# A planned instruction order laid out again, with separate hold and result times: cross-covariance attention followed by a channel mix

## The chip, the cores and the metric

One core of a Trainium2 chip runs the whole kernel. The metric is the device time of one execution in microseconds (us); lower is better. Three runs of the kernel before gave a median of 528.32 us (528.12 to 529.24).

## The reference

Cut to what matters, with B = 4, N = 6208, C = 256 and a hidden width of 1024:

```python
# attention over channels: per batch a 256 x 256 matrix
qn = q / (norm(q, axis=1) + 1e-6);  kn = k / (norm(k, axis=1) + 1e-6)
a  = softmax(kn.T @ qn / tau)
x  = v @ a
# channel mix
xk = mu_k * x + (1 - mu_k) * x_prev      # x_prev: x one row later, zero at row 0
xr = mu_r * x + (1 - mu_r) * x_prev
out = sigmoid(xr @ w_r) * (relu(xk @ w_k) ** 2 @ w_v)
```

The matrix `a` of a batch needs all rows of q and k of that batch, so the covariance of a batch must be complete before the first row of its x can be computed.

## The kernel before

The kernel does not issue instructions as its loops go. It first writes a list of steps with `add(engine, duration, key, function, reads, writes)` (class `Plan`). A step depends on the last writer of what it reads and on the readers of what it overwrites. Then `Plan.order()` lays all steps out in a small model of the machine: at each point the engine that can start first takes, of its steps whose inputs are there, the one with the lowest key. The keys say when a step is due: block n has its due time around n * T. The steps are then issued in the order of their modelled starts, and each engine runs its own list strictly in that order on the chip.

In the model of before a step holds its engine for one duration, and its result is there when that duration is over, plus a wait that depends on the engine that uses it (`WAIT`: PE 0.3, ACT and DVE 0.12, POOL 0.15). The durations are `act(n) = 0.17 + n/1200`, `dve(n) = 0.16 + n/960/mode`, `pe(n) = n/2400 + 0.0025`.

The work is tiled as follows. Batch 0 is special: its q and k come in as float32 over SP's queue (`ld0`, L280), DVE casts them (L291), ACT or DVE squares them (L300, L297), and TensorE accumulates the covariance (`cov0`, L313, into `s_ps`) and the sums of squares (`nq0` L306, `nk0` L319, into `vr`). There `s0` is a ring of three squared tiles, and `rq` (L324, L239 to L267) turns the norm of q into a row of factors. The function `softmax` then makes the matrix: copy of the norm of k (L365), a power on POOL (L239), two small DVE steps (L241, L244), two products with `rq` (L372), two exponentials on ACT (L386), and the two halves of `A` (L391, L393).

After that the kernel runs over 49 blocks, 48 of them of 512 rows (one of 256 holds the rests of the four batches). Each block goes through these steps:

- v is loaded by POOL's queue as bf16 (`v_load`, L335, ring `v_bf` of four) and transposed, the first five blocks on TensorE (`v_turn_pe`, L351, copied by DVE at L353), the others by a DMA on SP's queue (`v_turn_dma`, L341).
- `x_stage`: four matmuls of 512 columns make x in two halves (L427, into `xp`), each evacuated into `xR`, mostly by ACT (L437).
- `mix_stage` on DVE: difference `dl` (L467), products with mu `dm` (L475), sums `xk` and `xr` (L484).
- `up_stage`: four pairs of hidden tiles, each pair four matmuls of 512 columns (L513) into one of the two buffers `kT`; ACT takes the relu of the pair (L516, into `kr`, a ring of three), DVE squares it (L518, into `kk`).
- `down_stage`: for each 128 rows two gate matmuls (L546) and eight down matmuls (L551) into one of the two buffers `vr`; ACT takes a tanh (L555), DVE multiplies (L557), SP's queue stores (L571).

Between the blocks of one batch the covariance of the next batch is accumulated (`cov_group`): q and k are loaded by POOL's queue as bf16 (L622), ACT squares both at once (`sq`, L634, 128 x 2048), DVE adds twice (L637, L640), TensorE makes the covariance (`cov`, L650) and the sums (`norm`, L657), DVE adds these up (L664).

Of the kernel before, what the change touches and what calls it, by code (L numbers as in the profile page):

```python
# [13 lines left out]
OP = mybir.AluOpType  # L14
# [3 lines left out]
class Step:  # L18
    __slots__ = ("eng", "dur", "out", "key", "fn", "deps", "users", "left", "ready", "start", "seq", "size", "name")


class Plan:
# [3 lines left out]
    WAIT = {"PE": 0.3, "ACT": 0.12, "DVE": 0.12, "POOL": 0.15, "SP": 0.0}  # L26

    def __init__(self):
        self.steps = []
        self.writer = {}  # L30
        self.readers = {}

    def add(self, eng, dur, key, fn, reads=(), writes=(), size=0, name="", after=()):
        s = Step()
        s.eng, s.dur, s.key, s.fn, s.size, s.name = eng, dur, key, fn, size, name
        s.seq = len(self.steps)
        s.deps, s.users = set(after), []
        for r in reads:
            if r in self.writer:
                s.deps.add(self.writer[r])  # L40
            self.readers.setdefault(r, []).append(s)
        for w in writes:
            if w in self.writer:
                s.deps.add(self.writer[w])
            for r in self.readers.get(w, ()):
                s.deps.add(r)
            self.writer[w] = s
            self.readers[w] = []
        s.deps.discard(s)
        self.steps.append(s)  # L50
        return s

    RATE = 395e3
    MOVE = 1.3
    LAND = 0.8

    def order(self):
        import heapq
        for s in self.steps:
            s.left = len(s.deps)  # L60
            s.ready = 0.0
            for d in s.deps:
                d.users.append(s)
        free = {e: 0.0 for e in self.WAIT}
        waiting = {e: [] for e in self.WAIT}
        able = {e: [] for e in self.WAIT}
        bus = 0.0
        for s in self.steps:
            if s.left == 0:
                heapq.heappush(waiting[s.eng], (0.0, s.seq, s))  # L70
        done = []
        while len(done) < len(self.steps):
            best = None
            for e in free:
                if able[e]:
                    t = free[e]
                elif waiting[e]:
                    t = max(free[e], waiting[e][0][0])
                else:
                    continue  # L80
                if best is None or t < best[0]:
                    best = (t, e)
            t, e = best
            while waiting[e] and waiting[e][0][0] <= t:
                _, q, s = heapq.heappop(waiting[e])
                heapq.heappush(able[e], (s.key, q, s))
            s = heapq.heappop(able[e])[2]
            s.start = t
            end = t + s.dur
            free[e] = end  # L90
            if s.size:
                bus = max(bus, end + self.MOVE) + s.size / self.RATE
                end = bus + self.LAND
            s.out = end
            done.append(s)
            for u in s.users:
                lag = 0.0 if s.size else (0.02 if u.eng == e else self.WAIT[e])
                u.ready = max(u.ready, end + lag)
                u.left -= 1
                if u.left == 0:  # L100
                    heapq.heappush(waiting[u.eng], (u.ready, u.seq, u))
        done.sort(key=lambda s: (s.start, s.seq))
        return done


def pe(n):
    return n / 2400 + 0.0025


def act(n, ptr=0):  # L110
    return 0.17 + n / 1200 + 0.09 * ptr


def dve(n, mode=1):
    return 0.16 + n / 960 / mode
# [3 lines left out]
def kernel(  # L119
# [89 lines left out]
    T = 9.7  # L209
# [26 lines left out]
    def inverse(i, key, srcn, sres, lo, hi, name):  # L236

        nres = ("nq" if lo == 0 else "nk", i)
        add("POOL", 0.8, key + .01, lambda: nc.gpsimd.tensor_tensor(nrm[i][:, lo:hi], srcn[:, lo:hi], half[:, lo:hi], op=OP.pow),  # L239
            reads=[(sres, i)], writes=[nres], name=name + " pow")  # L240
        add("DVE", dve(4), key + .02, lambda: nc.vector.tensor_scalar_add(nrm[i][:, lo:hi], nrm[i][:, lo:hi], 1e-6),  # L241
            reads=[nres], writes=[nres], name=name)
        rw = [("rrq", i)] if hi == 2 else [("rrk", i)] if lo == 2 else [("rrq", i), ("rrk", i)]
        add("DVE", dve(4), key + .03, lambda: nc.vector.reciprocal(rr[i][:, lo:hi], nrm[i][:, lo:hi]),  # L244
            reads=[nres], writes=rw, name=name)
        if inv_tau != 1.0 and hi == 4:
            add("DVE", dve(4), key + .03, lambda: nc.vector.tensor_scalar_mul(rr[i][:, 2:4], rr[i][:, 2:4], inv_tau),
                reads=[("rrk", i)], writes=[("rrk", i)], name=name)

    def spread(i, key, name):  # L250
# [3 lines left out]
        add("DVE", dve(2), key + .04, lambda: nc.vector.tensor_copy(h, rr[i][:, 0:2]), reads=[("rrq", i)], writes=w, name=name)  # L254
        add("DVE", dve(2), key + .05, lambda: nc.vector.tensor_tensor(rd[i], rr[i][:, 0:2], h, op=OP.subtract),
            reads=[("rrq", i)] + w, writes=[("rd", i)], name=name)
        add("DVE", dve(2), key + .06, lambda: nc.vector.tensor_copy(m, rd[i]), reads=[("rd", i)], writes=w, name=name)
        add("DVE", dve(2), key + .07, lambda: nc.vector.tensor_tensor(l, rd[i], m, op=OP.subtract),
# [7 lines left out]
        add("PE", 6 * pe(P), key + .08, go, reads=w, writes=[("xp",)], name=name)  # L266
# [5 lines left out]
    for i, (tn, g, j0, j1) in enumerate(order0):  # L272
# [29 lines left out]
        if tn == "q":  # L302
            for j in range(j0, j1):
# [4 lines left out]
                add("PE", 0.13, key + 0.3, go, reads=[("s0", si)], writes=[("vr", 1)], name="nq0")  # L308
        else:
            for j in range(j0, j1):  # L310
# [4 lines left out]
                add("PE", 2 * pe(C), key + 0.1, go, reads=[cres, ("q0", g % NQ0)], writes=[("s_ps",)], name="cov0")  # L315
# [5 lines left out]
                add("PE", 0.16, key + 0.2, go, reads=[("s0", si)], writes=[("vr", 0)], name="nk0")  # L321
        if tn == "q" and g == NB:
            kq = key + 0.6
            add("DVE", dve(2), kq, lambda: nc.vector.tensor_copy(nrm[0][:, 0:2], vr[1][:, 0:2]),  # L324
                reads=[("vr", 1)], writes=[("nq", 0)], name="rq")
            inverse(0, kq, nrm[0], "nq", 0, 2, "rq")
            spread(0, kq, "rq")
# [11 lines left out]
    def v_turn_dma(n, key):  # L339
# [3 lines left out]
            reads=[("v_bf", i)], writes=[("vT", o)], size=M * C * 8, name="turn v")  # L343

    def v_turn_pe(n, key, pb, other=None):
# [6 lines left out]
        add("PE", 8 * 0.06, key, go, reads=[("v_bf", i)], writes=[pb[1]] + ([other] if other else []), name="turn v")  # L352
# [9 lines left out]
    def softmax(b, key, s_key):  # L362
        i = b % 2
        if b == 0:
            add("DVE", dve(2), key, lambda: nc.vector.tensor_copy(nrm[i][:, 2:4], vr[0][:, 0:2]),  # L365
# [14 lines left out]
        for ih in range(2):  # L380
# [7 lines left out]
            add("ACT", act(C, 1) + 0.19, key + .13 + .01 * ih, go, reads=[("rrk", i), ("mx", i)],  # L388
                writes=[("e", i, ih), ("sm", i, ih)], name="chain exp")
        for ih in range(2):  # L390
            add("DVE", dve(2), key + .15 + .01 * ih, lambda ih=ih: nc.vector.reciprocal(sm[i][:, ih:ih + 1], sm[i][:, ih:ih + 1]),  # L391
                reads=[("sm", i, ih)], writes=[("sm", i, ih)], name="chain")
            add("DVE", dve(C, 1.5), key + .155 + .01 * ih, lambda ih=ih: nc.vector.tensor_scalar_mul(  # L393
# [12 lines left out]
    def x_stage(n, key):  # L406
# [11 lines left out]
        for ci, (c0, c1) in enumerate(cuts):  # L418
            for dh in range(2):
# [11 lines left out]
                def both(go=go, kx=kx, w=c1 - c0, dh=dh, c0=c0, c1=c1, dst=dst, dres=dres):  # L431
                    add("PE", 2 * pe(w), kx, go, reads=[("A", b, 0), ("A", b, 1), ("vT", o)], writes=[dres], name="x")
# [8 lines left out]
    def mix_stage(n, key):  # L441
# [6 lines left out]
        for c0, c1 in cuts:  # L448
# [20 lines left out]
            unit(kd, lambda dgo=dgo, kd=kd, w=w: add("DVE", dve(2 * w, 2) + (.16 if left else 0), kd, dgo, reads=xdep,  # L469
                                                    writes=[("dl", di)], name="delta"))  # L470
            for which in "kr":
                km = kd + (.02 * T if which == "k" else .3 * T)
                for dh in range(2):
                    col = dh if which == "k" else 2 + dh
                    unit(km, lambda col=col, dh=dh, c0=c0, c1=c1, km=km, w=w: add("DVE", dve(w, 4), km, lambda: nc.vector.tensor_scalar_mul(  # L475
# [10 lines left out]
                unit(km + .01, lambda mgo=mgo, km=km, w=w, res_=res_: add("DVE", dve(2 * w, 2) + (.16 if left else 0), km, mgo,  # L486
# [16 lines left out]
    def up_pair(n, p, c0, c1, w, ku):  # L503
        def go():
# [3 lines left out]
            for x in range(2):  # L508
# [6 lines left out]
                marks[n] = add("PE", 2 * pe(w), ku + x * .02, mm, reads=[("w_k",), ("xk", n % 2, c0)], writes=[("kT", bk, x)], name="up")  # L515
# [19 lines left out]
    def down_tile(n, s, kd, last):  # L535
# [3 lines left out]
        def go():  # L539
# [7 lines left out]
            add("PE", 2 * pe(D), kd, gate, reads=[("xr", ri), ("w_r",)], writes=[("vr", bk)], name="gate")  # L547
            for p in range(4):
# [4 lines left out]
                add("PE", 2 * pe(D), kd + .01 * p, dn, reads=[("kk", n % 2, p, c0), ("w_v",)], writes=[("vr", bk)], name="down")  # L553
# [3 lines left out]
            add("DVE", 0.15 + D / 960, kd + .4, lambda: nc.vector.scalar_tensor_tensor(  # L557
# [24 lines left out]
    def left_stage(b, key):  # L582
# [13 lines left out]
        def both():  # L596
            add("PE", 4 * pe(65), kl, go, reads=[("A", b, 0), ("A", b, 1), ("vlT", i)], writes=[("xp",)], name="x left")
# [15 lines left out]
    def cov_group(b, g, key, dk):  # L613
# [12 lines left out]
        def work():  # L626
# [20 lines left out]
            for s in range(n):  # L647
# [4 lines left out]
                add("PE", 2 * pe(C), key + s * dk, go, reads=both, writes=[("s_ps",)], name="cov")  # L652
# [6 lines left out]
            add("PE", 0.3, kn, go, reads=[wres], writes=[("xp",)], name="norm")  # L659
            ai = b % 2  # L660
            if g == 0:
                add("DVE", dve(4), kn + .1, lambda: nc.vector.tensor_copy(acc[ai], xp[:, 0:4]), reads=[("xp",)], writes=[("acc", ai)], name="norm")
            else:
                add("DVE", dve(4), kn + .1, lambda: nc.vector.tensor_tensor(acc[ai], acc[ai], xp[:, 0:4], op=OP.add),  # L664
# [24 lines left out]
    add("DVE", dve(4), KC + .01, lambda: nc.vector.tensor_copy(mu, vr[1][:, 0:4]), reads=[("vr", 1)], writes=[("mu",)], name="mu")  # L689
# [83 lines left out]
```

## Time and profile before

| what | value |
|---|---|
| median of three runs | 528.32 us |
| span of the profiled execution, first to last instruction | 526.0 us |
| median of the runs less the span | 2.3 us |
| TensorE (PE) busy | 491.1 us, 93% of the span |
| VectorE (DVE) busy | 417.8 us, 79% |
| ScalarE (ACT) busy | 398.5 us, 76% |
| GpSimd (POOL) busy | 88.7 us, 17% |
| share of the chain of work that ended last that lies on PE | 77% |

How to read it: the span runs from the first to the last instruction of one execution, and some 2.3 us of the measured time lie around it. A matmul's busy time reaches to the arrival of its result, and the next matmul starts before that; so the busy share of PE is not its distance from its best rate. What counts is where PE waited, for what, and what the granted clock was. The profiled execution's own total time is not given beside its span; where a time of the whole kernel is worked out from the span, the 2.3 us are added.

### The profile page before, as it was taken

How to read it: one execution, taken by the hardware profiler on the slowest of the kernel's cores; microseconds unless marked ns; L12 is line 12 of the kernel's file. 1: busy time of each engine (PE TensorE's matmuls, PEld its weight loads, DVE VectorE, ACT ScalarE, POOL GpSimd, SP SyncE). 2: the span in 40 equal slices, each digit the busy share in tenths (PEclk: the TensorE clock that was granted, in tenths of full speed). 3: DMA queues.
4: the chain of work that ended last, by engine and by line, in shares of the span. 5: the costliest groups of instructions: out<-in, count | busy, mean ns of one | idle time of the engine just before them, and what ended most of it. 6: DMA issues, size and time to landing. Idle time of an engine off the chain costs nothing.

```text
span 526.0 us, 9943 instructions
## 1 busy us (share of the span) xinstructions
PE 491.1 (93%) x3707; PEld 342.7 (65%) x3761; DVE 417.8 (79%) x970; ACT 398.5 (76%) x573; POOL 88.7 (17%) x148
## 2 busy tenths in 40 slices
PE   1785999999899999999999999999999999999996
PEld 1563777756567767666667776666666666666674
DVE  4565997788879877798888778798888887878873
ACT  6543999788789978877898868877776787777763
POOL 0054433331123233211111210010010100000000
PEclk9998999999999999999999999999999999999999
DMA  8999999999999999998758854556465563413123
GB/s 333 402 312 206 205 187 203 197 203 206 212 191 133 205 188 161 210 215 128 127 106 145 147 90 92 126 102 145 97 99 143 105 143 81 121 40 102 41 81 100
DMA packets 113944, 83.23 MB, mean 158 GB/s; under 512 B 49572, under 2 KB 101352, under 8 KB 113896
## 3 DMA queue, kind: packets, MB, share of 16 engines
q0 software_dynamic: 38160, 33.01, 43.1%
q1 hardware_dynamic: 75736, 49.59, 36.5%
q8 instruction: 29, 0.48, 0.4%
q14 instruction: 19, 0.16, 0.1%
HBM read 78.71 MB, written 25.43 MB: 198 GB/s over the span
## 4 chain that ended last, share of the span: by engine, by line
PE 77%; DVE 7%; DMA 7%; issue 4%; ACT 3%; POOL 2%; SPq 0%; ACTq 0%; POOLq 0%
PE vr L551 28%; PE kT L513 28%; PE vr L546 7%; PE xp L427 6%; PE s_ps L650 6%; DMA f32s<-in_q_dram 3%; ACT kr L516 2%; DMA f32s<-in_k_dram 2%; DMA vT<-v_bf 2%; DVE kk L518 2%; DVE dm L475 1%; DVE res L557 1%; DVE dl L467 1%; DVE xk L484 1%; POOL v_bf L335 1%
## 5 line engine op out<-in xcount | busy, mean ns | idle before, releaser
L551 PE MATMUL vr<-w_v,kk 128*128 128x256 bf16 x1552 | 251.3, 273 | 1.0
L516 ACT ACTIVATE kr<-kT 128x1024 bf16<-128x1024 f32 (+1 forms) x200 | 198.6, 1001 | 53.2 <-PE kT L513 48.3
L513 PE MATMUL kT<-xk,w_k 128*128 128x512 bf16 (+1 forms) x746 | 213.4, 372 | 7.5 <-DVE xk L484 4.5
L551 PEld LDWEIGHTS <-kk 128*128 128x128 bf16 x1552 | 149.2, 98 | 83.8 <-issue 0.4
L518 DVE TENSOR_TENSOR kk<-kr 128x1024 bf16<-128x1024 bf16 (+1 forms) x200 | 134.7, 674 | 49.2 <-ACT kr L516 47.2
L555 ACT ACTIVATE res<-vr 128x256 f32<-128x256 f32 x194 | 74.1, 387 | 37.6 <-PE vr L551 35.1
L513 PEld LDWEIGHTS <-w_k 128*128 128x128 bf16 x800 | 77.6, 98 | 33.3 <-issue 5.0
L557 DVE SCALAR_TENSOR_TENSOR res<-res,vr 128x256 f32<-128x256 f32 x194 | 80.4, 417 | 18.2 <-ACT res L555 17.2
L546 PE MATMUL vr<-w_r,xr 128*128 128x256 bf16 x388 | 72.7, 272 | 2.5 <-DVE res L557 2.2
L634 ACT ACTIVATE sq<-f32s 128x2048 bf16<-128x2048 bf16 (+1 forms) x39 | 70.8, 1816 | 0.0
L335 POOL DMA_DIRECT2D v_bf<-in_v_dram x48 | 36.8, 766 | 197.4 <-DMA vT<-v_bf 170.3
L475 DVE TENSOR_SCALAR dm<-dl,mu 128x512 bf16<-128x512 bf16 (+1 forms) x200 | 62.4, 349 | 0.6
L437 ACT CAST xR<-xp 128x512 bf16<-128x512 f32 x94 | 55.3, 589 | 7.7 <-PE xp L427 7.2
L427 PE MATMUL xp<-vT,A 128*128 128x512 bf16 x188 | 56.9, 385 | 0.1
L546 PEld LDWEIGHTS <-xr 128*128 128x128 bf16 x388 | 37.7, 98 | 19.7 <-issue 3.8
L650 PE MATMUL s_ps<-f32s 128*128 128x256 bf16 (+1 forms) x294 | 48.8, 272 | 0.1
L467 DVE TENSOR_TENSOR dl<-xR 128x1024 bf16<-128x1024 bf16 (+1 forms) x49 | 33.1, 677 | 9.2 <-ACT xR L437 9.2
L300 ACT ACTIVATE s<-f32s 128x1024 bf16<-128x1024 f32 (+3 forms) x23 | 21.1, 926 | 18.3 <-DMA f32s<-in_q_dram 9.1
L622 POOL DMA_DIRECT2D f32s<-in_q_dram x39 | 21.1, 541 | 74.0 <-ACT res L555 15.1
L484 DVE TENSOR_TENSOR xk<-dm,xR 128x1024 bf16<-128x1024 bf16 (+1 forms) x49 | 33.2, 678 | 0.3
L484 DVE TENSOR_TENSOR xr<-dm,xR 128x1024 bf16<-128x1024 bf16 (+1 forms) x49 | 33.2, 677 | 0.3
L650 PEld LDWEIGHTS <-f32s 128*128 128x128 bf16 (+1 forms) x294 | 28.0, 97 | 4.7 <-issue 0.6
(68 smaller groups left out, 237.5 us busy)
## 6 DMA issues: line engine op xcount, KB each, us to landing
out_dram<-res SPq DMA_DIRECT2D x47, 512.0 KB, 3.7
v_bf<-in_v_dram POOLq DMA_DIRECT2D x48, 256.0 KB, 6.6
f32s<-in_q_dram POOLq DMA_DIRECT2D x36, 256.0 KB, 9.6
f32s<-in_k_dram POOLq DMA_DIRECT2D x36, 256.0 KB, 9.8
f32s<-in_q_dram SPq DMA_DIRECT2D x12, 512.0 KB, 7.7
f32s<-in_k_dram SPq DMA_DIRECT2D x11, 512.0 KB, 9.5
vT<-v_bf SPq DMA_TRANSPOSE x43, 3.9
w_k<-in_moe_w_k_dram POOLq DMA_DIRECT2D x1, 512.0 KB, 8.6
```

The costliest lines, as they stand in the source:

```text
L427: nc.tensor.matmul(dst, A[b][:, ih, dh * P:(dh + 1) * P], vT[o].rearrange("p (s h) q -> p h s q", h=2)[:, ih, c0 // P:c1 // P, :], start=i ...
L475: unit(km, lambda col=col, dh=dh, c0=c0, c1=c1, km=km, w=w: add("DVE", dve(w, 4), km, lambda: nc.vector.tensor_scalar_mul(dm[di][:, dh, c0 ...
L484: nc.vector.tensor_tensor(o[which][:, :, c0:c1], dm[di][:, :, c0:c1], xR[:, :, at + c0:at + c1], op=OP.add)
L513: nc.tensor.matmul(kT[bk][:, x, :w], w_k[:, dh, fh * P:(fh + 1) * P], xk[n % 2][:, dh, c0:c1], start=dh == 0, stop=dh == 1)
L516: add("ACT", act(2 * w), ku + .1, lambda: nc.scalar.activation(kr[kri][:, :, :w], kT[bk][:, :, :w], AF.Relu, scale=0.5 ** 0.5), reads=[("k ...
L518: add("DVE", dve(2 * w, 2), ku + .2, lambda: nc.vector.tensor_tensor(kk[n % 2][:, 2 * p:2 * p + 2, c0:c1], kr[kri][:, :, :w], kr[kri][:, : ...
L546: nc.tensor.matmul(V[:, D:], xr[ri][:, dh, s * P:(s + 1) * P], w_r[:, dh, :], start=dh == 0, stop=dh == 1)
L551: nc.tensor.matmul(V[:, :D], kk[n % 2][:, fh, s * P:(s + 1) * P], w_v[:, fh, :], start=fh == 0, stop=fh == 7)
L555: add("ACT", act(D), kd + .3, lambda: nc.scalar.activation(r[:, s], V[:, D:], AF.Tanh, scale=0.5), reads=[("vr", bk)], writes=[("res", oi, ...
L557: add("DVE", 0.15 + D / 960, kd + .4, lambda: nc.vector.scalar_tensor_tensor(r[:, s], r[:, s], 1.0, V[:, :D], op0=OP.add, op1=OP.mult), re ...
L634: add("ACT", act(w), key, lambda: nc.scalar.activation(Q[:rows, :, :n], G[:rows, :, :n], AF.Square), reads=both, writes=[("sq", si)], name ...
L650: nc.tensor.matmul(s_ps[:, ih, :], G[:rows, 1, s, ih * P:(ih + 1) * P], G[:rows, 0, s, :], start=g == 0 and s == 0 and ih == 0, stop=g == ...
```

## The change

The steps, their keys' formulas and their dependencies stay as they are; so do all tiles, buffers and instructions. What changes is the model that orders them:

- A step has two times now: `occ`, for which it holds its engine, and `lat`, after which its result is there. A user on the same engine may start when the engine is free; a user on another engine waits for `lat` and a short `HOP`.
- New times: a relu of 1024 elements holds ACT for 0.91 instead of 1.02 us, a square of 1024 holds DVE for 0.60 instead of 0.69, a step of four elements holds DVE for 0.07 instead of 0.16. The hop to PE is 0.06 instead of 0.3.
- The DMA model has one bus for SP's queue and one for POOL's, and a transfer of a transpose is priced at 4.6 bytes per element instead of 8.
- `T`, from which the keys are worked out, is 9.6 instead of 9.7.
- Code that could put filler matmuls into the order is added, but nothing sets `fill`, so none is made.

The core of the diff:

```diff
-    WAIT = {"PE": 0.3, "ACT": 0.12, "DVE": 0.12, "POOL": 0.15, "SP": 0.0}
+    HOP = {"PE": 0.06, "ACT": 0.04, "DVE": 0.04, "POOL": 0.1, "SP": 0.05}
+    RATE = 400e3
+    MOVE = 1.1
+    LAND = 1.1
...
-            end = t + s.dur
-            free[e] = end
+            free[e] = t + s.occ
+            end = t + s.lat
             if s.size:
-                bus = max(bus, end + self.MOVE) + s.size / self.RATE
-                end = bus + self.LAND
+                at, took = max(bus[e], end + self.MOVE), s.size / self.RATE
+                if e == "SP" and bus["POOL"] > at:
+                    bus["POOL"] += took
+                    took *= 2
+                bus[e] = at + took
+                end = bus[e] + self.LAND
...
-                lag = 0.0 if s.size else (0.02 if u.eng == e else self.WAIT[e])
-                u.ready = max(u.ready, end + lag)
+                r = free[e] if u.eng == e and not s.size else end + self.HOP[u.eng]
+                u.ready = max(u.ready, r)
...
-def pe(n):
-    return n / 2400 + 0.0025
-def act(n, ptr=0):
-    return 0.17 + n / 1200 + 0.09 * ptr
-def dve(n, mode=1):
-    return 0.16 + n / 960 / mode
+def pe(n, k=1):
+    one = n / 2400 + 0.0025
+    return k * one, (k - 1) * one + n / 2400 + 0.165
+def act(n):
+    occ = 0.06 + n / 1200
+    return occ, occ + 0.11
+def dve(n, mode=1.0):
+    occ = 0.07 + n / 960 / mode
+    return occ, occ + 0.085
...
-    T = 9.7
+    T = 9.6
...
-            reads=[("v_bf", i)], writes=[("vT", o)], size=M * C * 8, name="turn v")
+            reads=[("v_bf", i)], writes=[("vT", o)], size=M * C * 4.6, name="turn v")
```

Every engine's list is reordered by this. Of PE's 1815 steps 1612 stand at another place than before, of ACT's 564 steps 391, of DVE's 964 steps 744, of POOL's 142 steps 75, of SP's 128 steps 34.

## The prediction

> **What bounds the kernel now.** I read the page first, then the busy time by stage, then PE's waits and the chain of waits where PE stood still. The page:
>
> ```profile
> PE 491.1 (93%) x3707; PEld 342.7 (65%) x3761; DVE 417.8 (79%) x970; ACT 398.5 (76%) x573; POOL 88.7 (17%) x148
> ```
>
> The busy time of each engine by stage (length, then busy us and count for PE, PEld, DVE, ACT, POOL, then the granted clock, the DMA share and GB/s):
>
> ```profile
> 42.00:47.00 5.00, 1.59 (x13) 1.04 (x13) 2.68 (x9) 1.10 (x5) 3.83 (x7) 0.95 1.29 206
> 47.00:60.00 13.00, 10.78 (x84) 7.88 (x83) 10.78 (x31) 10.02 (x14) 6.03 (x11) 0.89 1.19 207
> 60.00:108.00 48.00, 47.63 (x370) 34.09 (x375) 40.18 (x91) 42.18 (x54) 17.58 (x31) 1.00 1.19 196
> 108.00:156.00 48.00, 44.57 (x322) 29.13 (x325) 39.99 (x93) 39.03 (x58) 8.30 (x14) 1.00 1.26 209
> 396.00:444.00 48.00, 46.77 (x327) 32.02 (x331) 40.21 (x92) 35.18 (x59) 4.47 (x6) 1.00 0.52 114
> ```
>
> From 60 to 492 us PE is idle for 0.37, 3.43, 0.36, 0.83, 0.43, 0.72, 0.87, 1.23 and 0.31 us in the nine stages of 48 us: 8.55 us in 432. So PE bounds the blocks, an order can't remove matmuls, and at most these 8.55 us and the drains hidden in them are to be had there. In the chain of waits sixteen L551 follow each other in 1.75 us and six L513 in 1.29, so 0.109 us for 256 columns and 0.215 for 512, while a lone matmul takes 0.273 and 0.379: each wait costs 0.164 us more than its idle time shows. With some 20 waits (13 stand in the list below; the shorter ones are my estimate) that is 3.3 us, in all 11.9. (The Trainium skill, "Perfetto Trace Analysis", section Identifying the Most-Contended Engine, would have TensorE's headroom judged by the share of LDWEIGHTS, not by matmul busy time. That share is 65% here and would leave a third of the span open; the idle times above leave 2%, and I go by them.)
>
> PE's waits from 60 to 492 us (waiting instruction, releaser, us in total, times, longest):
>
> ```profile
> PE kT L513 <- DVE xk L484: 3.0, 7, 0.8
> PE vr L546 <- DVE res L557: 1.5, 4, 0.6
> PE kT L513 <- ACT kr L516: 0.6, 1, 0.6
> PE xp L657 <- ACT xR L437: 0.5, 1, 0.5
> ```
>
> The first up pair waits for xk, which comes by PE x, ACT L437, DVE L467, L475, L484. No wait of PE there ends on a DMA.
>
> The second place is the turn from batch 0's covariance to the blocks, 3.41 us idle in 42 to 47 and 2.22 in 47 to 60. The chain there (start, us, what):
>
> ```profile
> 42.75 0.72 POOL nrm L239
> ...
> 43.90 0.61 ACT e_sb L386 x2
> ...
> 44.73 0.45 DVE A L393
> 45.18 0.07 DVE sm L391
> 45.25 0.59 DVE vT L353
> 45.84 0.42 DVE A L393
> 46.26 0.05 issue
> 46.30 0.67 PE kT L427 x3
> ```
>
> A copy of vT that nobody needs yet stands between the halves of A. A little later ACT's list shows squares for the next batch between the relus that PE waits for:
>
> ```profile
> 51.85 1.09 ACT L516 ACTIVATE kr<-kT 128x512 bf16<-128x512 f32 x2 [1.49 <-PE kT L513]
> 52.82 1.91 ACT L634 ACTIVATE sq<-f32s 128x2048 bf16<-128x2048 bf16 x1
> 54.62 1.08 ACT L516 ACTIVATE kr<-kT 128x512 bf16<-128x512 f32 x2
> 55.58 1.93 ACT L634 ACTIVATE sq<-f32s 128x2048 bf16<-128x2048 bf16 x1
> ```
>
> **Part 1, the turn (30 to 60 us).** I compared the instruction lists of the two orders. To the end of batch 0's loads they nearly agree. Then:
> - The six matmuls of rq (L264, 37.27 to 37.61) move ahead of the last k tiles, where PE waited 0.49 for a cast anyway, and the first eight transposes L351 (41.15 to 41.59) move behind the last L319. The sums of k are complete 0.34 + 0.44 = 0.8 us earlier.
> - The norm copy L365 (42.52) moves ahead of the second product L372 and of the vT copy; it can follow the sums by 0.2, at about 41.3 instead of 42.5. The chain to A starts 1.2 us earlier.
> - The vT copy L353 (0.59) moves behind the second half of A, so x starts 1.2 + 0.6 = 1.8 us earlier.
> - DVE takes both halves of block 0's mix ahead of block 1's difference (0.6 of hold) and two squares (0.34 each): the second half's xk comes a further 1.3 us earlier. ACT takes the first square (1.9 us) behind six relus, not behind two.
> - Against it: POOL's power now stands ahead of one k load (L622, issued at 36.26). The power waits for its input until 41.3, so the load is issued 6 us later, at about 42.3; with 9.8 us to landing it is there at 52. Behind it in POOL's queue stand the loads of the next groups, which before went out at 43.43, so they lose nothing. But seven covariance steps (0.218 each, 1.5 us) that filled PE's waits between 52.9 and 56 are not there then.
>
> Sum: 1.8 + 1.3 - 1.5 = 1.6 us, plus a little for the relus: I take 2.0. Bounds: 0.3, if only the 1.8 less the lost filling counts, and 3.5, if the filling was free.
>
> A rule speaks against this part. PE idles in 42 to 47 and the granted clock falls to 0.89 in the next 13 us, 1.4 us of clock lost. In the new order PE's gaps of 0.82, 1.98 and 0.78 become one of about 3 us. By the Trainium skill, "TensorE: Matmul & The Clock Gate", Part 1: The HAM clock gate, a window of about 3.4 us without work halves the clock; by that rule one more such window would cost up to 1.7 us. The row shows the low clock already there with shorter gaps, so I count no change, and 1.4 us as the bound on either side.
>
> **Part 2, the blocks (60 to 492 us).** With 0.109 and 0.215 per matmul I counted, in both lists, how much PE work stands between a producer on PE and the PE instruction that needs what ACT and DVE make of it. The need comes from the rows: for x to up 0.16 drain + 0.59 (L437) + 0.69 (L467) + 0.61 (two L475) + 0.69 (L484) and some 0.2 of hand-overs, 2.9 us. In the order of before the cover exceeds the need by 2.04 us in the median, in the new one by 0.74. Places where it falls short: 7 with 2.6 us in all before, 19 with 5.4 us after. So the new order has 2.8 us more of waits that no queue causes.
>
> Of the 8.55 us idle before, 2.6 are of that kind, and 6.0 come from queues on ACT and DVE: results were late although PE had work enough in between. The old model held ACT 1.02 us for a relu where two back to back take 1.94, so 0.91 each; for DVE it held 0.69 against 0.60. With 0.11 too much for each of a block's 4 relus, 2 evacuations and 4 tanh, the old model held ACT 1.1 us too long per block, and its order was wrong about what is late. The new model has the trace's numbers here. I take three quarters of the 6.0 as gone, 4.6; bounds none and all. The sum of part 2 is 4.6 - 2.8 = 1.8 us gained (from 2.8 lost to 3.2 gained).
>
> **DMA, the queues.** Twenty v loads move ahead of two to ten q/k loads in POOL's queue. A v load waits for the transpose that frees its buffer; the longest such wait is 16.6 us, and the q/k loads now stand behind it. In the trace POOL issued q and k of batch 2's tenth group at 121.16, while batch 1's power, which comes ahead of all of batch 2's covariance, ran at 155.46: 34 us of lead against 16.6, so I cost this at nothing. Without that cover a late group would cost PE up to 16.6 us once. vT gains lead by it; each transpose's issue ended at least 12.8 us ahead of its x matmul already. SP's stores and transposes swap places with neighbours only: nothing. The tail (5.02 us idle in 492 to 526) has the same last waits in both lists: nothing.
>
> **Sum.** 526.0 - 2.0 - 1.8 = 522.2 us of span, plus the 2.3 around it: 524.5 us.
>
> **The rivals.**
> 1. The waits go altogether: all 6.0 of queues and the 3.3 of drains, less the 2.8, and the turn gains 3.5 less 0.5 of clock: 6.5 + 3.0, so 518.8 us. For it: the new times agree with the rows to some hundredths. Against it: the thinner covers.
> 2. Slower: the thin cover breaks at the squares. In the new ACT list L634 (hold 1.8 us) stands directly ahead of an x evacuation 16 times (10 before) and of a relu 16 times (8 before). If PE's order does not cover these 14 further places, each costs half a hold, 0.9 us: 12.6 us; at half of the places 6.3, in place of part 2's gain, less the 2.0 of the turn: 532.6 us. It decides from 5 places on (4.5 us against the 3.8 gained). For it: a margin of 0.74 is less than half a hold. Against it: the new model holds ACT 1.77 us for a square, where the row has 1.91 less 0.11, so PE's order allows for nearly all of it.
> 3. No change: the second low-clock window (1.4) and part 2 at its middle (+0.2) leave 528.0 us.
>
> **How the numbers follow.** Forecast (524.5, by itself 521.5 to 527): 0.46. Waits go (518 to 521): 0.20. Slower: 0.23. No change: 0.11. A measurement of this kernel can tell about 0.2%, 1.06 us, from no change. Faster is 0.46 + 0.20 = 0.66, same 0.11, slower 0.23. The range from 518.5 to 530.5 leaves out half of the slow case and a little of the fast one.
>
> **What would show it.** Right: the first x matmul near 44.5 us instead of 46.3, A's halves next to each other, idle in 42 to 60 down from 5.6 to under 4, and idle in 108 to 156 well under 3.4. Part 2 is wrong if PE's idle time in 60 to 492 is above 8.55 with L513 waiting for xk more than 7 times; rival 2 shows as waits of L513 and L546 behind L634. A wait of PE on a DMA would show the queues costed wrongly.

## The result and the profile after

Before 528.22 us (median of four runs, 527.71 to 529.24), after 545.77 us (median of four). Two executions of after took 535.98 and 536.98 us and two took 554.56 and 562.04; the comparison is made with the first two, and the profile shown here is that of the 554.56 us execution. The ratio is 1.0161, 95% interval 1.0136 to 1.0186: after is slower by some 8 us. The forecast was 524.5, so its sign was wrong.

Span 552.8 us. The lines of the page on the engines and on the chain that ended last:

```profile
PE 505.8 (92%) x3761; PEld 343.9 (62%) x3761; DVE 426.6 (77%) x970; ACT 402.1 (73%) x573; POOL 88.7 (16%) x148
...
PE 55%; DMA 20%; DVE 14%; issue 5%; ACT 4%; POOL 1%; SPq 0%; ACTq 0%; POOLq 0%
```

Before, the chain lay on PE for 77%, on DVE for 7% and on transfers for 7%. DVE has the same 970 instructions and is busy for 426.6 us, where it was for 417.8. That line is easy to pass over, and it turned out to be the mark of the loss. (Line numbers: those of after and of e9 to e19 are 23 higher than those of before for the same statement, in e10 19; e1 to e8 and e17 have before's.)

The busy time by stage, columns as in the prediction:

```profile
42.00:47.00 5.00, 2.25 (x22) 1.60 (x19) 2.83 (x11) 1.47 (x5) 4.10 (x8) 0.82 1.28 201
47.00:60.00 13.00, 10.82 (x82) 7.48 (x80) 11.90 (x33) 8.93 (x13) 5.77 (x10) 0.94 1.16 195
60.00:108.00 48.00, 47.49 (x369) 33.01 (x366) 41.28 (x93) 43.92 (x56) 15.02 (x26) 1.00 1.31 173
108.00:156.00 48.00, 40.02 (x275) 25.66 (x274) 32.11 (x72) 29.94 (x43) 7.25 (x12) 0.93 1.35 149
396.00:444.00 48.00, 46.34 (x332) 30.34 (x330) 40.69 (x99) 33.04 (x54) 5.34 (x7) 1.00 0.59 116
```

In 108 to 156 PE stands idle for 7.98 us (3.43 before). The chain of waits shows what happened there in this execution (start, us, what):

```profile
112.38 14.48 DMA out_dram<-res
...
126.94 0.04 ACT res L578
...
127.22 0.59 ACT xR L460
```

A store issued at 112.38 lands 14.48 us later; ACT's tanh, which writes the same one of the three `res` buffers, waits for it, the x evacuation L460 stands behind it in ACT's list, and PE's x behind that. In all ACT waits 14.0 us in three places on stores (`ACT res L578 <- DMA out_dram<-res`; 1.4 before). This is not the 8 us between the two kernels, as e7 shows.

### The profile page after: what moved, and what is told of

Its sections match the earlier page's. It is cut to its first block, busy times and chain, and to the rows that moved or that the text cites. A ratio compares the mean times of both kernels' runs of the same rounds, so it can differ in the third digit from the quotient of the medians.

```text
span 552.8 us, 10008 instructions
## 1 busy us (share of the span) xinstructions
PE 505.8 (92%) x3761; PEld 343.9 (62%) x3761; DVE 426.6 (77%) x970; ACT 402.1 (73%) x573; POOL 88.7 (16%) x148
## 4 chain that ended last, share of the span: by engine, by line
PE 55%; DMA 20%; DVE 14%; issue 5%; ACT 4%; POOL 1%; SPq 0%; ACTq 0%; POOLq 0%
PE kT L536 20%; PE vr L574 20%; DMA vT<-v_bf 10%; DMA out_dram<-res 5%; PE vr L569 5%; PE xp L450 4%; PE s_ps L673 3%; DMA f32s<-in_q_dram 3%; DVE dm L498 3%; DVE kk L541 2%; DMA f32s<-in_k_dram 2%; DVE dl L490 2%; PE s_ps L336 2%; DVE xk L507 2%; ACT kr L539 1%
## 5 line engine op out<-in xcount | busy, mean ns | idle before, releaser
L574 PE MATMUL vr<-w_v,kk 128*128 128x256 bf16 x1552 | 216.3, 273 | 3.5 <-DVE kk L541 3.1
L536 PE MATMUL kT<-xk,w_k 128*128 128x512 bf16 (+1 forms) x800 | 202.5, 376 | 4.5 <-DVE xk L507 2.6
L578 ACT ACTIVATE res<-vr 128x256 f32<-128x256 f32 x194 | 74.3, 390 | 44.0 <-PE vr L574 26.9
L580 DVE SCALAR_TENSOR_TENSOR res<-res,vr 128x256 f32<-128x256 f32 x194 | 78.8, 415 | 18.8 <-ACT res L578 18.5
L569 PE MATMUL vr<-w_r,xr 128*128 128x256 bf16 x388 | 74.4, 274 | 4.5 <-DVE res L580 4.5
L460 ACT CAST xR<-xp 128x512 bf16<-128x512 f32 x94 | 55.5, 590 | 19.5 <-PE xp L450 18.9
L673 PE MATMUL s_ps<-f32s 128*128 128x256 bf16 (+1 forms) x294 | 44.7, 278 | 1.1 <-DVE e_sb L395 1.1
L490 DVE TENSOR_TENSOR dl<-xR 128x1024 bf16<-128x1024 bf16 (+1 forms) x49 | 33.2, 678 | 11.5 <-ACT xR L460 11.2
L450 PEld LDWEIGHTS <-A 128*128 128x128 bf16 x196 | 19.3, 100 | 21.4 <-issue 7.8
```

The lines of the kernel that those rows point to most:

```text
L450: nc.tensor.matmul(dst, A[b][:, ih, dh * P:(dh + 1) * P], vT[o].rearrange("p (s h) q -> p h s q", h=2)[:, ih, c0 // P:c1 // P, :], start=i ...
L536: nc.tensor.matmul(kT[bk][:, x, :w], w_k[:, dh, fh * P:(fh + 1) * P], xk[n % 2][:, dh, c0:c1], start=dh == 0, stop=dh == 1)
L569: nc.tensor.matmul(V[:, D:], xr[ri][:, dh, s * P:(s + 1) * P], w_r[:, dh, :], start=dh == 0, stop=dh == 1)
L574: nc.tensor.matmul(V[:, :D], kk[n % 2][:, fh, s * P:(s + 1) * P], w_v[:, fh, :], start=fh == 0, stop=fh == 7)
L578: add("ACT", act(D), kd + .3, lambda: nc.scalar.activation(r[:, s], V[:, D:], AF.Tanh, scale=0.5), reads=[("vr", bk)], writes=[("res", oi, ...
L580: add("DVE", dve(D), kd + .4, lambda: nc.vector.scalar_tensor_tensor(r[:, s], r[:, s], 1.0, V[:, :D], op0=OP.add, op1=OP.mult), reads=[("v ...
```

## The experiments

Every kernel was timed in alternation with before on its chip. A list is an engine's sequence of instructions; where a kernel takes lists from both orders, or has buffers changed under a fixed order, the planner's answer is replaced by a written one:

```diff
-    seq = plan.order()
+    seq = [plan.steps[i] for i in ORDER]
```

**Whose lists are to blame?** Three theories: Q, POOL's list; S, SP's list; C, thin covers in the lists of PE, ACT and DVE (the prediction's second rival was one form of C). Both orders have the same steps and dependencies, so POOL's and SP's lists can be exchanged.

e1: PE, ACT and DVE as in before, POOL and SP as in after.

> PE's, ACT's and DVE's lists of before, POOL's and SP's lists of after. Theory Q (POOL's list: v loads ahead of q/k loads keep transposes and loads in each other's way, stores land late, ACT's tanh waits for res): 533 to 545 us, with ACT waiting for stores by several us. Theory S (SP's list: two transposes ahead of two stores): the same. Theory C (thinner covers in PE's list, queues without part in it): 528 us as before.

529.84 us, ratio 1.0031 (1.0014 to 1.0048); one of ten executions took 551.06. In the other nine the queues of after cost 1.6 us on the compute lists of before, not 8.

e2: PE, ACT and DVE as in after, POOL and SP as in before.

> PE's, ACT's and DVE's lists of after, POOL's and SP's lists of before. Q and S: the loss is gone, 522 to 527 us (the prediction's 524.5 for the compute lists alone), no wait of ACT for a store over 2 us. C: still 535 us or more.

557.36 us, ratio 1.0556 (1.0538 to 1.0573). So the compute lists carry the loss, and queues laid out for other lists make it worse. ACT waits on stores (`ACT res L555 <- DMA out_dram<-res: 22.2, 2, 11.5`), and the waits of SP's queue show why they are late (waiting instruction, releaser, us in total, times, longest):

```profile
SPq L341 <- DMA v_bf<-in_v_dram: 126.5, 11, 35.8
...
SPq L586 <- DMA vl<-in_v_dram: 27.5, 2, 25.5
```

A transpose that waits for its v load holds the stores behind it in SP's queue.

e3: all lists of after, POOL's of before.

> All lists of after but POOL's, which is that of before. Q: 522 to 527 us. S: 534 or more, since SP's list is still that of after. C: 535 or more.

570.27 us median, four executions from 557.65 up; the wait on stores is 35.4 us. Q alone falls, as far as lists that don't belong together can tell.

e4: all lists of after, SP's of before.

> All lists of after but SP's, which is that of before. Q: 533 to 545 us, since POOL's list is still that of after. S: 522 to 527. C: 535 or more.

543.01 us, ratio 1.0253 (1.0178 to 1.0329). S alone falls as well, with the same reserve.

**What in the compute lists?** In after PE's list holds the covariance matmuls of batches 1 to 3 back: the last of batch 1 stands behind output tile 30, before behind 18. A q or k load waits for its buffer until the covariance has read it, so POOL issues the loads of batch 2's second to tenth group from 93 to 161 us in the trace of after and from 85 to 121 in that of before. Theory K made this the cause, theory R the ring of three `res` buffers.

e5: the lists of after, 123 covariance steps put ahead in PE's list.

> The lists of after, on all five engines, with one edit in PE's: 123 of the 147 covariance matmul steps of batches 1 to 3 (L650 in before's numbering) stand ahead of their place, after the same gate or down step that they follow in before. In after they stand up to 22 output tiles later than in before (the last of batch 1 behind tile 30 where before has it behind tile 18), so that the f32s slots come free later and POOL's q/k loads of batch 2 go out between 93 and 161 us where before sends them between 85 and 121 us. Theory K (the late covariance is the loss, through f32s slots and the in-order queues): 526 us, between 522 and 530; the q/k loads of batch 2 are out by 125 us, and ACT's wait on stores of res falls from 14.0 us to under 4. Theory C (thin covers between x, delta, mix and up in the new compute lists, wherever the covariance stands): 536, between 533 and 540, with ACT's store wait as long as in after. Theory R (only the ring of three res buffers): between 530 and 540, as the stores still stand behind the transposes in SP's list.

550.62 us, ratio 1.042 (1.0399 to 1.0441), with no wait on stores. PE now waits for xk 17 times, 7.7 us in all: the steps that filled its waits have gone ahead.

e6: the lists of before, with the covariance as late as in after.

> The reverse: the lists of before on all five engines, with the 147 covariance matmul steps of batches 1 to 3 moved in PE's list to stand after the same gate or down step that they follow in after; nothing else moves. Theory K: at least 6 us slower than before, 534 to 550, with the q/k loads of batch 2 out only around 160 us and store waits on ACT above 10 us. Theory C: within 1.5 us of before (528), since every other step of the compute lists is before's. Theory R: in between, only as far as stores happen to be held.

555.65 us, ratio 1.0507 (1.0461 to 1.0553). One gap makes up half of it:

```profile
POOL f32s L622 <- PE s_ps L650: 42.3, 4, 26.5
...
PE vr L546 <- DVE res L557: 20.6, 14, 13.8
```

The place of the covariance does matter for the queues, but in both directions a class of steps moved by hand spoils an order that was laid out as a whole. K is neither shown nor excluded by these two.

e7: the order of after, six `res` buffers.

> The lists of after unchanged, with six res buffers instead of three, so that ACT's tanh waits for the store of six blocks back and not of three. Theory R: the 14 us wait of ACT on stores goes and with it the loss: 526 to 529. Theory K: the waits on stores go (about 6 to 8 us at PE), but the late loads still hold up the v loads and transposes behind them, so part stays: 528 to 533. Theory C: 533 to 537.

```diff
-    res = ring("res", 3, [S, D], F32)
+    res = ring("res", 6, [S, D], F32)
...
-        ri, oi = n % 3, n % 3
+        ri, oi = n % 3, n % 6
```

536.03 us, all four executions between 535.45 and 537.09; ratio 1.0139 (1.0123 to 1.0156). No wait of ACT on a store is left, and the 8 us are all there. With six buffers none of four executions is long, but the ratio stays: R explains no part of it. This kernel shows the loss undisturbed; PE's waits from 60 to 492 us in it:

```profile
PE kT L513 <- DVE xk L484: 2.9, 6, 1.5
PE xp L657 <- DVE rq L267: 1.6, 2, 0.9
...
PE s_ps L650 <- DVE e_sb L372: 1.1, 2, 0.6
```

PE waits no more for xk than in before (3.0 us, 7 times).

e8: the order of after, 14 buffers for q and k loads instead of 10 (batch 0 keeps ten).

> The lists of after unchanged, with 14 f32s buffers for the q/k loads of batches 1 to 3 instead of 10 (batch 0 keeps its ten), so that a load waits for the covariance of 14 groups back and POOL's list no longer stands on late covariance matmuls. Theory K: the loss goes without a matmul being moved: 524 to 530, POOL's q/k loads of batch 2 out about 15 to 25 us earlier than in after. Theory C: 533 to 540. Theory R: as after, 533 to 540.

535.70 us, ratio 1.0134 (1.0117 to 1.0151). Loads that no longer wait for late covariance bring nothing back: K falls.

**Which line of the model?** The rest mostly undoes one part of the source change and lets the planner lay out a new order. Theory M: the short waits and holds of the model make it optimistic, so that it keeps the covariance back. (Its own end is 516.5 us for after; the planner of before expects 542.1.)

e9: the waits between engines as in before.

> The source of after with one line put back: the waits from engine to engine in the model are before's (PE 0.3, ACT 0.12, DVE 0.12, POOL 0.15, SP 0.0 us) and not 0.06, 0.04, 0.04, 0.1 and 0.05; the hold and result times, the two transfer buses and T stay as in after. The model's own end goes from 516.5 to 537.0 us, and it then puts the last covariance matmul of batches 1, 2 and 3 behind output tiles 20, 63 and 111, near before's 18, 63 and 108, where after has 30, 83 and 129. Theory M (a model with waits near nothing keeps the covariance back as if no gap needed filling, so that PE stands at each softmax and DVE sets the pace there): 526 to 530. Theory Q+S (transfers and queues): 533 to 540, as the transfer model is after's. Theory C (thin covers everywhere): 530 to 535.

548.02 us, ratio 1.0382 (1.0347 to 1.0417).

e10: the transfer model as in before.

> The source of after with only the model of transfers put back to before's: one bus for SP and POOL, 395 KB per us, 1.3 and 0.8 us around it, and the turn of a v block counted as M*C*8 bytes. The covariance stays late (behind tiles 26, 83 and 129). Theory M: 533 to 540, as after. Theory Q+S: back to 527 to 530, since the lists of POOL and SP and all that hangs on their transfers are then laid out by before's prices. Theory C: 533 to 540.

546.91 us, ratio 1.0345 (1.0318 to 1.0372). In this order PE waits on a transpose itself (`PE xp L446 <- DMA vT<-v_bf: 4.9, 1, 4.9`), as in e9 (3.0 us).

e11: the times of ACT and DVE as in before.

> The source of after with before's longer times for ACT and DVE (0.17 and 0.16 us a step beside the columns, the same for hold and result), the short waits and all else as in after. The model's end goes to 540.1 us and the covariance early again (last ones behind tiles 18, 57 and 113). Theory M: 526 to 531, by a second way than the waits. Theory Q+S: 533 to 540. Theory C: 528 to 533, since DVE and ACT covers get longer as well.

554.15 us, ratio 1.0504 (1.0458 to 1.055), of which PE waits 10.1 us in one place behind a store. The covariance is early in e9 and e11 and the loss is larger, so M's forecast fails; these totals also hold waits on transposes and stores, and the place of the loss, below, says more.

e12: a step that needs the step before it on its own engine starts at that step's result, not when the engine is free.

> The source of after with one expression changed: a step that needs the result of the step before it on the same engine starts at that step's result time in the model, and not when the engine is free. In the trace of the kernel with six res buffers the six small DVE steps of batch 1's softmax, each needing the one before, took 158.26 to 159.45 us, 1.19 us, where the model of after gives them 0.5 us. The model's end goes from 516.5 to 521.2 us; the covariance stays late (31, 80 and 121). Theory M: little regained, 531 to 536. A theory that the loss is the small dependent DVE steps mis-sized at each softmax: 527 to 530.

```diff
-                r = free[e] if u.eng == e and not s.size else end + self.HOP[u.eng]
+                r = end if u.eng == e and not s.size else end + self.HOP[u.eng]
```

531.47 us, ten executions from 527.18 to 536.49, ratio 1.0033 (0.9999 to 1.0067). One expression brings back most of the loss. Which engine's rule is it?

e13: the same for DVE alone, `r = (end if e == "DVE" else free[e]) if ...`; six `res` buffers.

> The model of after with the same-engine rule changed for DVE alone (a DVE step that needs the DVE step before it starts at that step's result, not when DVE is free), its order run with six res buffers, so that waits on stores play no part; the base is after with six res buffers, 536.0 us. Theory L-DVE (the loss is DVE's chain of dependent steps at the softmaxes of batches 1 to 3, laid out 0.09 us a step too tight): 527 to 531, with PE's idle time at the softmaxes under half of the 8 us. Theory L-PE (the gain of the run with the rule changed on all engines came from PE's own order): 534 to 537. Theory M (covariance late): 534 to 537, since it stands at tiles 33, 81 and 131.

527.18 us, ratio 0.9988 (0.9960 to 1.0016), against 536.03 for e7.

e14: the same for PE alone; six `res` buffers.

> The model of after with the same-engine rule changed for PE alone (a PE step that needs the PE step before it, as the four parts of down do, starts 0.165 us later in the model, so that other work is laid between), its order run with six res buffers. L-DVE: 534 to 537. L-PE: 527 to 532. M: 533 to 537 (covariance ends behind tiles 28, 80 and 129).

541.98 us, ratio 1.0246 (1.0194 to 1.0298). L-PE falls, L-DVE stands as to the cause of the loss; where its gain lies is another matter, below.

e15: the order of e12, six `res` buffers.

> The order of the run with the same-engine rule changed on all engines (531.5 us, single runs from 527.2 to 536.5), with six res buffers instead of three. If the spread of that run is waits on stores, as in after: 526.5 to 528.5 with all runs within 1.5 us of one another; it would then be level with before or a little faster. If the spread is anything else, it stays at 527 to 536.

532.48 us, executions from 527.45 to 538.63: the spread of this order is not the wait on stores. In the profiled execution (533.49) PE waits once for 3.5 us on a transpose.

e17: the control, before with six `res` buffers.

> Before with six res buffers, its order unchanged: the control for the runs with six. ACT waited on a store once for 1.4 us in before, so all theories expect 527.5 to 529.

528.21 us, ratio 0.9998 (0.9982 to 1.0014).

e18: the order of e13, eight buffers each for v and its transpose.

> The order of e13 (same-engine result times for DVE alone, six res buffers) with eight buffers each for v and for its transpose instead of four, so that POOL's list does not stand for 150 us on transposes (POOL v_bf <- DMA vT<-v_bf: 151.0 us in e13). If the spread of e13's executions (525.2 to 531.3 us) comes from transposes and v loads that are late in some executions: 525 to 526.5 with all of them within 1.5 us, faster than before by 0.4 to 0.6%. If more loads in flight run into the transposes and stores: 528 to 535. If the spread is neither: 527, as e13.

529.59 us, ratio 1.0015 (0.9994 to 1.0036), executions from 526.11 to 535.95: more buffers don't take the spread of e13 (525.18 to 531.32) away. In the profiled execution of e18, its slowest, PE waits 8.2 us in four places on transposes; what spreads these orders from one execution to the next stays open.

e19: after with the one condition of e13 and nothing else.

> The order of e13 with three res buffers, as in after: against after this is one condition in the model and nothing else. Theory L-DVE: 526 to 532 in the executions without a wait on stores. If a store is held behind a transpose, as in two of the four executions of after, single executions reach 540 to 560.

526.28 us, ratio 0.9969 (0.9949 to 0.9989). With one condition the new model's order is some 10 us faster than with it missing (1.0161 / 0.9969 = 1.019), and a little faster than before.

**What the condition does in the lists.** Counted in the orders themselves, a DVE step stands directly behind a DVE step whose result it needs 61 times in before, 216 times in after and 96 times in e13 and e19 (204, 215 and 202 times in e9, e10 and e11, 193 in e14). Before's model added 0.02 us to a same-engine dependency, so a step that was able already came first; after's has nothing there, both are able at one time, and the key, which puts the chain of one block together, decides. (In e11 the result is there when the hold ends, and the neighbours are still 202: the tie is enough.) DVE's timeline in e7 ahead of batch 1's softmax (start, us, what), a difference, its products and sums, each waiting for the one before (the second pair of products because it overwrites `dm`):

```profile
152.93 0.69 DVE L467 TENSOR_TENSOR dl<-xR 128x1024 bf16<-128x1024 bf16 x1
153.65 0.62 DVE L475 TENSOR_SCALAR dm<-dl,mu 128x512 bf16<-128x512 bf16 x2
154.31 0.69 DVE L484 TENSOR_TENSOR xk<-dm,xR 128x1024 bf16<-128x1024 bf16 x1
155.03 0.62 DVE L475 TENSOR_SCALAR dm<-dl,mu 128x512 bf16<-128x512 bf16 x2
155.68 0.69 DVE L484 TENSOR_TENSOR xr<-dm,xR 128x1024 bf16<-128x1024 bf16 x1
```

And in e19 a few us on, where other steps stand between:

```profile
158.84 0.68 DVE L541 TENSOR_TENSOR kk<-kr 128x1024 bf16<-128x1024 bf16 x1
159.44 0.69 DVE L490 TENSOR_TENSOR dl<-xR 128x1024 bf16<-128x1024 bf16 x1
160.04 0.68 DVE L541 TENSOR_TENSOR kk<-kr 128x1024 bf16<-128x1024 bf16 x1
160.64 0.42 DVE L290 COPY rq<-xp 128x256 f32<-128x256 f32 x1
160.98 0.34 DVE L498 TENSOR_SCALAR dm<-dl,mu 128x512 bf16<-128x512 bf16 x1
```

Read the distance from start to start: 0.72 from the difference to the product that needs it, 0.60 from square to difference to square. A step's result comes after 0.69, the next independent step starts after 0.60. Over the whole trace of e7 the difference holds DVE 0.728 us in the median where its product follows directly (35 places; 11 in before) and 0.603 elsewhere; a product ahead of its sum holds it 0.382 (95 places; 17 in before), elsewhere 0.268. That is 24 x 0.125 + 78 x 0.114 = 11.9 us more on DVE's list than in before. Busy time shows less of it, 8.8 us, since DVE counts as idle from a step's own end to its dependent successor's start (some 0.03 us each). The pages agree, the first line that of e7, the second that of e19:

```profile
PE 501.3 (94%) x3761; PEld 342.7 (64%) x3761; DVE 426.6 (80%) x970; ACT 402.1 (75%) x573; POOL 89.0 (17%) x148
```

```profile
PE 491.8 (93%) x3712; PEld 343.0 (65%) x3761; DVE 416.9 (79%) x970; ACT 399.8 (76%) x573; POOL 89.6 (17%) x148
```

All orders laid out without the condition for DVE have DVE busy for 422 to 428 us, those with it, and those on before's compute lists, for 414 to 419.

## Why the prediction was wrong

Idle time of PE is a poor guide here: between 60 and 444 us it is 8.24 us in before and 9.36 in e7, and yet e7 is 8 us longer, because each short wait also shows a matmul's drain, which counts as busy. So I compared at equal work: the time at which PE had been given so many us of matmul columns (2400 columns counted as 1 us, as the planner's `pe` does; from the weight loads), less that work. Time beyond the work, us, to some 0.2, from the three profiles:

| matmul work, us | what lies there | before | e7 (order of after) | e19 |
|---|---|---|---|---|
| 0 to 24 | batch 0, the turn | 38.9 | 38.6 | 39.0 |
| 24 to 72 | blocks | 2.2 | 2.9 | 2.3 |
| 72 to 108 | blocks | 5.3 | 3.5 | 2.1 |
| 108 to 120 | batch 1's softmax | 1.0 | 3.8 | 3.2 |
| 120 to 216 | blocks | 4.0 | 5.7 | 3.1 |
| 216 to 252 | batch 2's softmax | 1.7 | 5.8 | 5.2 |
| 252 to 324 | blocks | 4.0 | 4.1 | 2.3 |
| 324 to 348 | batch 3's softmax | 2.0 | 3.2 | 2.2 |
| 348 to 456 | blocks without covariance | 2.2 | 2.0 | 1.9 |
| sum | | 61.3 | 69.6 | 61.3 |

Point by point:

- **Part 2, the queues of DVE: the step that failed.** "The new model has the trace's numbers here. I take three quarters of the 6.0 as gone, 4.6." The hold of 0.60 against 0.69 is right for a step whose successor is independent. I read it as a gain for all steps and did not ask what the model does with a successor that needs the result; the diff shows that line (`r = free[e] if u.eng == e`), and the lists that I had compared hold the 216 direct neighbours. DVE's list became 8.8 us longer in busy time, and the term of +4.6 became a loss: the five rows of blocks sum to 17.7 us in before and 18.2 in e7, where part 2 had 1.8 less. The gain forecast is there in one place, 5.3 to 3.5 at 72 to 108 us of work, and in the other blocks it is given back; with the condition, in e19, the five rows sum to 11.7, a gain of 6.0. That the condition is the cause is shown by e13 and e19 against e7 and after; that the lengthening of DVE's list is how it acts follows from the counts and the traces, since no kernel changed the neighbours alone.
- **The place, a term that the sum did not have.** Net of small gains and losses elsewhere, e7's excess over before lies at the softmaxes, 2.8 + 4.1 + 1.2 = 8.1 us, where DVE has the chain of the softmax on top of the blocks. The prediction said nothing on batches 1 to 3's softmaxes. My later expectation that the correction would halve the excess there was wrong too: of the 8.3 us between e7 and e19 only 2.2 lie at the softmaxes and the rest in the blocks between (6.5, less 0.4 at the turn). So e19 is level with before because 6.0 us gained in the blocks stand against 5.9 us still lost at the softmaxes. Late covariance does not explain that loss: e5 has it at before's places, with the other lists of after, and 3.7, 5.6 and 3.1 us in these three rows. At batch 1's softmax DVE sets the pace, and the new orders lay more of its work there: beside the same 12 us of matmul work it is busy 12.31 of 13.00 us in before (154.2 to 167.2), 14.79 of 15.80 in e7 (153.0 to 168.8) and 14.42 of 15.20 in e19 (151.4 to 166.6). At batch 2's, part of e19's 5.2 us comes from POOL's list: the last sum of the norms (DVE `acc`) ends at 273.10, and the power that waits for it starts only at 275.90, behind a v load whose buffer a transpose held:

```profile
261.80 12.79 DMA vT<-v_bf
...
275.14 0.76 POOL v_bf L358
275.89 0.01 issue
275.90 1.06 POOL nrm L262
```

  In e13, the same order, this delay is 1.4 us and the row 3.8. In e7 there is none; what makes its 5.8 there is not shown.
- **Part 2, the covers.** The 2.8 us for thinner covers from x to up did not come: PE waits for xk 2.9 us in e7, 3.0 before.
- **Part 1, the turn.** A's halves are next to each other as said, but the chain did not start earlier, and x came 0.6 us earlier and not 1.8:

```profile
42.09 0.41 DVE e_sb L395
42.50 0.07 DVE nrm L388
42.57 0.33 DVE e_sb L395
42.90 0.60 DVE vT L376
...
44.64 0.45 DVE A L416
45.09 0.07 DVE sm L414
...
45.19 0.44 DVE A L416
45.63 0.05 issue
45.68 0.84 PE kT L450 x3
```

  The norm copy (L388) starts at 42.50 as before, since the first product (L395), which waits for all of the covariance, stands ahead of it; I had only looked at the second. The turn's gain at 24 us of work is 0.3 us in e7 and some 1.2 in e8, not 2.0. What sets these two apart is the clock, not the order: by the rows of 42 to 47 and 47 to 60, before lost 5 x 0.05 + 13 x 0.11 = 1.7 us of clock; after (0.82 and 0.94) and e8 (0.89 and 0.91) lost 1.7 as well and e7 (0.71 and 0.85) 3.4, on the same compute lists. On before's own lists e17 (0.94 and 0.89) lost 1.7 and e1 (1.00 and 0.74) 3.4. So counting no change for the order holds, and what comes from one execution to the next comes in portions of 1.7. The rule that I had set aside (the Trainium skill, "TensorE: Matmul & The Clock Gate", Part 1: The HAM clock gate) has about that portion: a window of some 3.4 us at half the clock, by my estimate 1.7 us.
- **The queues, costed at nothing.** On before's compute lists they cost 1.6 us (e1). The prediction looked at the q and k loads that now stand behind v loads; in e1's trace it is batch 2's power that starts 3.3 us after its input was there, behind a v load, and the row of that softmax has 3.8 us, where before has 1.7. The forecast that PE would not wait on a transfer held in e7. With lists that don't belong together they cost up to 40 us (e2, e3).
- **Rival 2** had the sign right and the engine wrong: in e7 PE waits 1.5 us in one place on a relu, and for no evacuation behind a square.
- **Rival 3's sum** is off: 528.3 less 2.0, plus 1.4, less the 0.2 gained is 527.5, not 528.0. Nothing else rests on it.

## What to carry to other kernels

When an order is laid out by a model, check first what the model does with a dependent step on the same engine: a hold time measured between independent steps must not be used between dependent ones. Count the direct neighbours in the new list, and compare an engine's busy time over the same instructions: 2% more of it was the sign here. Compare two orders at equal work, not by idle time: the kernel can be level with before and still lose in one place what it gains in another. Lists taken from two orders, or steps moved by hand, can do worse than either whole order (e2 to e6; e1 came out between the two).

## What the runs showed of the hardware

A DVE step on 128x1024 bf16 lets an independent successor start after 0.603 us, ahead of its own end at 0.69, and a dependent one only after 0.728; on 128x512 with one tensor 0.268 and 0.382. The Trainium skill, "VectorE: DVE Perf Modes", section The DRAIN you can't avoid, measured eight copies with and without a semaphore after each and says that it costs nothing extra. In these runs a step that waits for the one before it starts about 0.12 us later than one that doesn't, and the measurement decides.

A store of 512 KB, which lands after some 4 us in the median, took 14.48 us in after and 16.18 us in e11, and a transpose up to 24.34 us in e10. Before has such landings too, stores up to 16.5 us and transposes up to 20.8, with 1.4 us of ACT's waits on stores: a late landing alone is not yet a cost.
